# A planned two-layer kernel: other transfer latencies in its planner, the first V rows behind the output weights, another stored order

## The chip, the cores and the metric

The kernel runs on one core of a Trainium2 chip. The metric is the device time of one execution in microseconds (us); the time given for a kernel is the median of several executions. A "profiled execution" is one execution taken by the hardware profiler; its span runs from the first to the last instruction, and every duration below comes from it.

## The reference

Four layers follow one another on a sequence x of 2048 rows of 512 numbers (bf16): A, B, A, B, each added to its input, each on a layer norm of it.

```python
# A: recurrent attention with a memory of 8 rows; 64 segments of 32 rows, 32 heads of 128
mem = mem0
for s in range(64):
    h = concatenate([mem, x[s*32:(s+1)*32]])          # 40 rows
    q, k, v = h @ Wq, h @ Wk, h @ Wv                  # 40 x 4096 each
    p = softmax(mask(q @ k.T * scale))                # 40 x 40 for each head
    o = (p @ v) @ Wo                                  # 40 x 512
    mem, out[s] = o[:8], o[8:]
# B: a gated feed-forward net (FFN) with 1792 hidden columns
out = (sigmoid(x @ w_gate) * (x @ w_up)) @ w_down
```

The new memory of a segment needs the whole segment before it, so layer A is a chain of 64 steps. Both A layers have the same weights, and both B layers too.

## The kernel before

**Steps and jobs.** The kernel runs the two A layers as two jobs, j = 0 and j = 1, with job 1 six segments behind job 0 (LAG). One step t computes segment t of job 0 and segment t - 6 of job 1 side by side, so that most matmuls have 80 columns (two times 40). There are 70 steps: steps 0 to 5 and 64 to 69 have one job alone. After each fourth step a block of 128 rows goes through the FFN (`ffn`).

**A step** (`emit_step`) goes through six groups of heads. For each: q and k (L926), copied to qku by ScalarE; the scores (L961); the softmax on VectorE and ScalarE (L975 to L992); a transpose of the probabilities (L1004), whose two halves are spread into ptsb by ScalarE or VectorE (L1008 to L1017); probabilities times V (L1030, "pv") into a bank; and the output product with wo_sb (L1048), which adds up in one bank over all groups. The last product gives the memory of the next step (L1061, L1066).

**V** comes by two ways into the tiles vsb, of which there are three, two for each step (8 head pairs each). Rows of x that are known early go through `v_pass` (L716) or `v_half` (L753) to a DRAM buffer scr, and are fetched back for the step as **V rows** (L895, vsb<-scr, 16 or 48 KB a transfer). Rows that depend on the memory, and some next to them, are computed in the step itself as **V strips** (`strips`, L840: 32 columns for all heads) and copied into the tile sst by ScalarE or VectorE; four or eight DMAs (L906, vsb<-sst) take them to vsb. L1030 needs rows and strips.

**Weights.** wq, wk, wv and wo (4 MB each) are loaded once at the start (L603), in pieces: wo_sb in twelve, two for each of six groups of heads, ten of 384 KB and two of 128 KB. The last of them, in program text, is that of head 31. The FFN weights don't stay; GpSimd (POOL) issues their loads of 256 KB (wg, wu, wd, L1142, L1143, L1167) for each block anew. All other DMAs are issued by SyncE (SP), in the order of its instruction stream: where one of them waits for a semaphore, all behind it wait.

**The order of everything** is a plan made on the host before the program is built. `Planner.add` enters each of 13,442 tasks (a few instructions each) with the engines that may run it, a duration, a latency until its result is there, and what it reads and writes. `forward` then runs through time: whenever an engine is free, it takes the ready task that stands first in a stored order (SEQUENCE, a packed permutation of all tasks). The starts that come out give each engine's instruction order. Nothing of the modelled times is in the program: an engine waits only for the real semaphores of its data. Two exceptions are made from the plan: FFN loads wait for the matmul task that ended last before their planned start (`pace`), and where the plan has TensorE idle for over 250 ns, matmuls on a tile of zeros are put in (L1273, `warm`), to keep its clock up; their number follows from the planned gap.

A transfer with a size (`nb`) is modelled by one shared bus: it is done at the later of the bus's end plus 1.2 us and the end of its issue plus `lat`. FFN loads (at least BIG bytes on POOL) start only when the modelled bus is nearly free.

Of the kernel before, what the change touches and what calls it, by code (L numbers as in the profile page):

```python
# [1352 lines left out]
```

## Time and profile before

| what | us |
|---|---|
| median of 3 runs | 1787.03 |
| lowest and highest | 1783.6, 1788.61 |
| the profiled execution, its own time | 1788.62 |
| its span, first to last instruction | 1786.8 |
| TensorE busy in it | 1757.7 |
| TensorE matmuls on zeros (L1273) in it | 25.3 |
| VectorE, ScalarE, GpSimd busy | 1178.8, 1155.2, 581.9 |

TensorE's granted clock was 0.997 of full speed over the span. The profile names an instruction by its line, its engine (PE is TensorE's matmul, PEld its weight load, DVE VectorE, ACT ScalarE, POOL GpSimd, SPq SyncE's queue of DMA issues) and the tiles that it writes and reads ("vsb<-sst"). "Waits" list, for an engine, the line that waited, what released it, the sum of the waits, their number and the longest. The "chain" is the work that ended last, followed back from the end; a DMA in it lasts from the end of its issue until its landing.

### The profile page before, as it was taken

To read this page: it belongs to the slowest core of one execution; us is meant where nothing else is said; L and a number is where in the kernel's file an instruction comes from. 1 tells how busy PE (TensorE), PEld (TensorE's weight loads), DVE (VectorE), ACT (ScalarE), POOL (GpSimd) and SP (SyncE) were. 2 spreads that over 40 slices of the span, in tenths; PEclk is the share of its full clock that TensorE was granted. 3 is DMA by queue.
4 is the path that set the end of the run, shared out by engine and by line. 5 is a ranking of instruction groups with operands and counts; after the bars stand their busy time and mean duration, and the time that the engine had idled before them with its cause. 6 is when DMAs were issued, how large, how long until landed. Compare 5 with 4: busy or idle time off the path is not lost.

```text
span 1786.8 us, 92278 instructions
## 1 busy us (share of the span) xinstructions
PE 1757.7 (98%) x40059; PEld 1511.0 (85%) x40059; DVE 1178.8 (66%) x4061; ACT 1155.2 (65%) x2981; POOL 581.9 (33%) x839
## 2 busy tenths in 40 slices
PE   9999999999999999999999999999999999999998
PEld 4588788889888898989898898889888888989886
DVE  4377666776677666766676667657766766766675
ACT  5676756676666666666666666666665766666664
POOL 5414031413233242323334241333324132333432
PEclk9999999999999999999999999999999999999999
DMA  9735354636455464445546463545546454554543
GB/s 351 242 96 162 96 158 132 191 106 169 137 162 156 129 174 139 138 136 163 160 139 187 130 181 102 154 145 165 156 138 173 115 159 128 156 154 133 171 140 99
DMA packets 135048, 273.42 MB, mean 153 GB/s; under 512 B 30826, under 2 KB 68594, under 8 KB 134642
## 3 DMA queue, kind: packets, MB, share of 16 engines
q0 software_dynamic: 56848, 183.55, 35.0%
q1 hardware_dynamic: 77794, 83.97, 16.3%
q8 instruction: 314, 5.14, 1.3%
q14 instruction: 92, 0.75, 0.1%
HBM read 221.78 MB, written 27.07 MB: 139 GB/s over the span
## 4 chain that ended last, share of the span: by engine, by line
PE 89%; DMA 5%; SPq 2%; issue 1%; ACT 1%; DVE 1%; POOL 1%; POOLq 0%; ACTq 0%; DVEq 0%
PE bank L926 31%; PE bank L1048 16%; PE bank L1150 10%; PE bank L840 7%; PE bank L716 7%; PE bank L1173 5%; PE bank L1030 4%; PE bank L961 4%; PE bank L1004 2%; DMA vsb<-sst 2%; SPq L906 2%; DMA wv_sb<-in_A_Wv_dram 1%; PE bank L676 1%; DMA wo_sb<-in_A_Wo_dram 1%; PE bank L1118 0%
## 5 line engine op out<-in xcount | busy, mean ns | idle before, releaser
L926 PE MATMUL bank<-hT,wq_sb 128*128 128x80 bf16 (+3 forms) x8960 | 616.7, 198 | 1.2 <-issue 1.1
L926 PE MATMUL bank<-hT,wk_sb 128*128 128x80 bf16 (+3 forms) x8960 | 616.2, 198 | 0.5 <-issue 0.5
L1287 ACT CAST qku<-bank 128x480 bf16<-128x480 f32 (+3 forms) x770 | 387.8, 507 | 219.8 <-PE bank L926 180.9
L926 PEld LDWEIGHTS <-wq_sb 128*128 128x128 bf16 x8960 | 452.5, 99 | 23.7 <-issue 13.6
L926 PEld LDWEIGHTS <-wk_sb 128*128 128x128 bf16 x8960 | 447.7, 99 | 1.2 <-issue 1.2
L975 DVE TENSOR_TENSOR st<-bank,cst 40x240 f32<-40x240 f32 (+3 forms) x768 | 279.3, 368 | 155.6 <-PE bank L961 149.4
L1048 PE MATMUL bank<-otsb,wo_sb 128*128 128x80 bf16 (+1 forms) x8960 | 362.3, 198 | 5.5 <-DMA wo_sb<-in_A_Wo_dram 3.3
L1048 PEld LDWEIGHTS <-wo_sb 128*128 128x128 bf16 x8960 | 336.3, 99 | 18.8 <-DMA wo_sb<-in_A_Wo_dram 3.7
L1143 POOL DMA_DIRECT2D wu<-in_B_w_up_dram x217 | 164.6, 759 | 276.2 <-PE bank L1150 86.9
L1287 ACT CAST otsb<-bank 128x480 bf16<-128x480 f32 (+3 forms) x420 | 199.0, 484 | 68.1 <-PE bank L1030 48.2
L1142 POOL DMA_DIRECT2D wg<-in_B_w_gate_dram x217 | 163.9, 756 | 240.3 <-PE bank L1150 92.1
L1167 POOL DMA_DIRECT2D wd<-in_B_w_down_dram x217 | 154.2, 711 | 197.0 <-PE bank L1173 46.3
L985 ACT ACTIVATE st<-st 80x240 f32<-80x240 f32 (+3 forms) x420 | 158.9, 381 | 44.4 <-DVE st L982 42.8
L666 POOL TENSOR_TENSOR small<-small,cst 128x1 f32<-128x1 f32 (+1 forms) x80 | 45.7, 573 | 404.5 <-DVE small L665 401.6
L987 DVE TENSOR_REDUCE small<-st 80x6 f32<-80x240 f32 (+3 forms) x420 | 151.0, 362 | 37.3 <-ACT st L985 34.4
L1150 PE MATMUL bank<-xnT,wg 128*128 128x128 bf16 (+2 forms) x1784 | 171.9, 219 | 0.0
L1150 PE MATMUL bank<-xnT,wu 128*128 128x128 bf16 (+2 forms) x1784 | 171.3, 218 | 0.0
L961 PE MATMUL bank<-qku 128*128 128x80 bf16 (+1 forms) x2240 | 163.2, 198 | 1.4 <-ACT qku L1287 1.2
L982 DVE TENSOR_TENSOR st<-st,small 80x240 f32<-80x240 f32 (+3 forms) x420 | 154.6, 370 | 4.0
L992 DVE TENSOR_TENSOR pb<-st,small 80x240 bf16<-80x240 f32 (+3 forms) x420 | 153.4, 369 | 4.0
L980 DVE TENSOR_REDUCE small<-st 80x6 f32<-80x240 f32 (+3 forms) x420 | 151.6, 363 | 4.5
L1030 PE MATMUL bank<-ptsb,vsb 104*128 104x80 bf16 x2048 | 136.7, 199 | 7.8 <-DMA vsb<-sst 6.1
(106 smaller groups left out, 2403.4 us busy)
## 6 DMA issues: line engine op xcount, KB each, us to landing
wg<-in_B_w_gate_dram POOLq DMA_DIRECT2D x220, 256.0 KB, 4.4
wu<-in_B_w_up_dram POOLq DMA_DIRECT2D x220, 256.0 KB, 4.3
wd<-in_B_w_down_dram POOLq DMA_DIRECT2D x220, 256.0 KB, 4.2
vsb<-scr SPq DMA_DIRECT2D x460, 48.0 KB
vsb<-sst SPq DMA_DIRECT2D x464, 32.0 KB
scr<-vst SPq DMA_DIRECT2D x112, 96.0 KB
wv_sb<-in_A_Wv_dram SPq DMA_DIRECT2D x8, 512.0 KB
wo_sb<-in_A_Wo_dram SPq DMA_DIRECT2D x10, 384.0 KB
```

The source lines that it names most:

```text
L926: nc.tensor.matmul(o_ap, lhsT=W[:, c, h * P:(h + 1) * P], rhs=mv(c), start=(c == 0), stop=(c == DC - 1))
L961: nc.tensor.matmul(s_all(SB)[:, w0 + i, :], lhsT=fview(qku[:, i, 0, 0:1], [(1, P)]), rhs=qku[:, i, 1, 0:ncol], start=True, stop=True)
L975: pl.add("DVE", dve_ns(n, True), lambda gsz=gsz, hs=hs, st=st, SB=SB, pj_=pj_, npj_=npj_, mk=mk, idx=idx: nc.vector.tensor_tensor(out=st[p ...
L982: pl.add("DVE", dve_ns(n), lambda gsz=gsz, hs=hs, st=st, mx=mx: nc.vector.tensor_tensor(out=st[pr, hs], in0=st[pr, hs], in1=mx[pr, hs].uns ...
L985: pl.add("ACT", act_ns(n), lambda hs=hs, st=st: nc.scalar.activation(out=st[pr, hs], in_=st[pr, hs], func=ACTF.Exp, scale=self.scale), r=s ...
L1030: nc.tensor.matmul(fview(OB[:, o:o + 1], [(ncol, 2), (1, L)]), lhsT=self.vsb[halves[u // 8]][0:64 + L, j, (u % 8) * P:(u % 8 + 1) * P], rh ...
L1048: nc.tensor.matmul(WB[:, c * ncol:(c + 1) * ncol], lhsT=self.wo[:, h, c * P:(c + 1) * P], rhs=otsb[:, hl, 0:ncol], start=(h == 0 and c == ...
L1142: pl.add("POOL", 760, lambda wg=wg, fs=fs: nc.gpsimd.dma_start(out=wg[:], in_=self.wgv[:, :, fs]), r=[("wo", self.H - 1)], w=[gk] + bt, la ...
L1143: pl.add("POOL", 760, lambda wu=wu, fs=fs: nc.gpsimd.dma_start(out=wu[:], in_=self.wuv[:, :, fs]), r=[("wo", self.H - 1)], w=[uk] + bt, la ...
L1150: nc.tensor.matmul(gu[:, 2 * i + k, 0:n], lhsT=W[:, c, i * P:(i + 1) * P], rhs=xnT[:, c, rw], start=(c == 0), stop=(c == DC - 1))
L1167: pl.add("POOL", 760, lambda wd=wd, ip=ip: nc.gpsimd.dma_start(out=wd[:], in_=self.wdv[:, 2 * ip:2 * ip + 2, :]), w=[dk] + (["boot"] if se ...
L1287: nc.scalar.copy(out=dst, in_=src)
```

## The change

The diff changes numbers of the planner, one dependency, and the stored order. No task is added or removed.

- A task has a new field `slow`. `forward` keeps `wbus`, the time until which the FFN loads under way occupy the bus, and adds `slow` times the rest of that (at most BACK, 2300 ns) to a transfer's latency.
- V rows: `lat` 4300 becomes 2425 with `slow` 1.0, so 2425 to 4725 ns. V strips: 3200 becomes 2800 with `slow` 0.6, so 2800 to 4180 ns.
- The V rows of step 0 also depend on the output weight load of head 31. This is a dependency of the plan: it decides where the rows stand on SP; the program has no wait for it.
- `warm`: TensorE counts as slow until 4400 ns instead of 8000, the first gap is counted from 1000 ns instead of 1200, and a gap is filled at 2.4 columns per ns for the part of it behind 4400 ns (before, 1.2 for every gap whose end lay before 8000 ns).
- The second half of the ptsb spread costs 52 ns more on VectorE in the plan.
- SEQUENCE is another permutation. Unpacked: 422 of the 13,442 places hold the same task; half of all tasks move by 13 places or fewer; among the first 1000 places the median move is 166, from place 3000 on it is 6 to 24. The twelve wo_sb loads stood at places 322 to 646 and stand at 170 to 520; the four V rows of step 0 stood at 356 to 572 and stand at 427 to 509; the V matmuls of the start (L716 on xvf) stood at 169 to 759 and stand at 68 to 548.

```diff
 SEQUENCE = r"""
...
 """
-    SPAN, COLD, WARM0 = 3413.0, 8000.0, 1200.0
+    SPAN, COLD, WARM0, BACK = 3413.0, 4400.0, 1000.0, 2300.0
...
-    def add(self, eng, dur, fn, r=(), w=(), lat=None, boost=0.0, use=(), late=0.0, nb=0):
+    def add(self, eng, dur, fn, r=(), w=(), lat=None, boost=0.0, use=(), late=0.0, nb=0, slow=0.0):
...
-        bus = 0.0
+        bus = wbus = 0.0
...
-                    done = max(bus + self.TAIL, end + tk.lat)
+                    done = max(bus + self.TAIL, end + tk.lat + tk.slow * min(max(wbus - now, 0.0), self.BACK))
+                    if e == "POOL" and tk.nb >= self.BIG:
+                        wbus = max(wbus, now + self.LEAD[e]) + tk.nb / self.BUS
...
-                cold = tk.start < self.COLD
+                cold = end < self.COLD
...
-                    n = int((gap - 120.0) * (1.2 if cold else 2.4)) // P
+                    n = int((gap - 120.0) * 2.4 - (min(tk.start, self.COLD) - end) * 1.2 * cold) // P
...
-                        r=[("vd", j, b, q, kk) for q in range(lo // 8, (lo + nx) // 8) for kk in (h0 // 4, h0 // 4 + 1)], w=[("vx", j, vh, i)], lat=4300.0, nb=nx * 2048)
+                        r=[("vd", j, b, q, kk) for q in range(lo // 8, (lo + nx) // 8) for kk in (h0 // 4, h0 // 4 + 1)] + ([("wo", self.H - 1)] if t == 0 else []), w=[("vx", j, vh, i)], lat=2425.0, nb=nx * 2048, slow=1.0)
...
-                        r=[(sb, 0), (sb, 1)], w=[(name, j, vh, i)], lat=3200.0, use=[sb], nb=nr * 2048)
+                        r=[(sb, 0), (sb, 1)], w=[(name, j, vh, i)], lat=2800.0, use=[sb], nb=nr * 2048, slow=0.6)
...
                 d["ACT"] += 93.0 * i
+                d["DVE"] += 52.0 * i
```

## The prediction

> **What bounds the kernel now.** I read the page's busy shares first, then the waits of PE (TensorE), then its timeline and clock around the longest wait, then SP's own timeline in that stretch, and last the chain of work at a late stall.
>
> ```profile
> span 1786.8 us, 92278 instructions
> PE 1757.7 (98%) x40059; PEld 1511.0 (85%) x40059; DVE 1178.8 (66%) x4061; ACT 1155.2 (65%) x2981; POOL 581.9 (33%) x839
> ```
>
> TensorE is busy for 1757.7 of 1786.8 us; VectorE and ScalarE are busy for two thirds. The matmuls of the reference are the same in both programs, so only two things can shrink: the 29.1 us in which TensorE is idle, and the warming matmuls of L1273 (25.3 us by the groups of lines: 9.2 us before 20 us, 8.9 us from 100 to 220 us, 4.3 us after 1650 us). Everything else can only be hidden better or worse.
>
> The waits of TensorE (engine, line, what released it: us in total, times, longest):
>
> ```profile
> PE bank L1030 <- DMA vsb<-sst: 6.1, 7, 2.0
> PE bank L1048 <- DMA wo_sb<-in_A_Wo_dram: 3.3, 1, 3.3
> PE bank L1118 <- ACT oxT L1287: 2.1, 6, 0.4
> PE bank L716 <- DMA wv_sb<-in_A_Wv_dram: 1.6, 1, 1.6
> ```
>
> Two are the change's subject: seven short waits for V strips over the whole run, and one wait for an output weight. By stretches, the idle time is 8.7 us before 110 us, 6.3 us from 120 to 300 us, 8.2 us from 300 to 1740 us, and 6.1 us at the end. The steady stage has hardly anything left.
>
> TensorE's timeline at the output weight (start, length):
>
> ```profile
> 80.04 0.26 PE L1048 MATMUL bank<-otsb,wo_sb 128*128 128x40 bf16 x4
> 83.61 1.12 PE L1048 MATMUL bank<-otsb,wo_sb 128*128 128x40 bf16 x28 [3.30 <-DMA wo_sb<-in_A_Wo_dram]
> 84.55 1.88 PE L716 MATMUL bank<-wv_sb,xvf 128*128 128x512 bf16 x4
> ```
>
> and busy time, granted clock, DMA share and GB/s of single microseconds there:
>
> ```profile
> 82.00:83.00 1.00, 0.00 (x0) 0.83 1.05 380
> 83.00:84.00 1.00, 0.39 (x12) 0.50 0.72 248
> 84.00:85.00 1.00, 1.00 (x24) 0.50 0.20 61
> 88.00:89.00 1.00, 1.00 (x28) 0.50 0.55 129
> 89.00:90.00 1.00, 1.00 (x36) 0.75 0.39 133
> ```
>
> The wait costs more than its 3.30 us: the clock falls to 0.50 and comes back only at about 89.5 us. SP's timeline says why the weight was late:
>
> ```profile
> 54.12 0.37 SPq L603 DMA_DIRECT2D wo_sb<-in_A_Wo_dram  x1
> 54.53 2.74 SPq L895 DMA_DIRECT2D vsb<-scr  x2
> 67.62 2.61 SPq L906 DMA_DIRECT2D vsb<-sst  x3
> 70.28 0.59 SPq L603 DMA_DIRECT2D wo_sb<-in_A_Wo_dram  x1
> 70.91 0.52 SPq L906 DMA_DIRECT2D vsb<-sst  x1
> 71.47 2.69 SPq L603 DMA_DIRECT2D wo_sb<-in_A_Wo_dram  x5
> ```
>
> SP issues in order. After the V rows it stands at a strip's DMA (L906) from 57.3 to 67.6 us until the strip is in sst; six of the twelve output weights are behind it. Meanwhile the DMA engines run empty: 0.99 busy in 50 to 60 us, 0.32 (99 GB/s) in 60 to 70 us.
>
> Last, the chain of work at the longest strip wait:
>
> ```profile
> 1155.02 0.59 SPq L906
> 1155.61 0.04 issue
> 1155.65 4.85 DMA vsb<-sst
> ```
>
> A strip took 4.85 us from the end of its issue; at the other stalls that the chain shows it took 4.47, 4.58 and 5.57 us. The plan of before reckons with 3.2 us.
>
> **Step 1: output weights ahead of the first V rows.** The four V rows of step 0 now depend, in the plan, on the load of heads 31; the program gets no wait by it, only another order on SP. In the stored order the twelve weight loads stood at places 322 to 646 and now stand at 170 to 520. The six late ones (6 issues, 0.59 + 2.69 = 3.28 us of SP) should then go out before SP blocks, by about 54.5 + 3.3 = 58 us. They are 2.0 MB (five of 384 KB, one of 128 KB, by the old order). At the 365 to 395 GB/s of the busy stretches that is 5.3 to 5.8 us, from about 60 us, when the DMA engines come free: landed near 66 us instead of 83.56. The need is at 76 to 80 us, so the 3.30 us go.
>
> The clock: after 83.61 us four matmuls of L716 take 1.67 us to the next group where they took 0.86 at 79.18 us (+0.81); 28 of L1048 take 0.94 where 0.71 is the warm pace of 24 in 0.61 (+0.23); the 18 pairs of L926 from 86.22 to 89.49 us take 3.27 where the warm pace later is 0.10 for a group of four, 1.8 in all (+1.45). Sum 2.5 us. Here the Trainium skill speaks against counting it: TensorE: Matmul & The Clock Gate, Part 1, has the clock fall after at least one idle window of about 3.4 us, and the wait was 3.30 us. By that rule only 3.30 us would be won; by the row, 3.30 + 2.5 = 5.8 us. The row decides, since it shows 0.50.
>
> What is late next is the V rows, moved behind six weight issues: four issues (1.9 us for four at 51.21 us) between 66 and 68 us at the earliest. The first L1030 comes at 74.86 us, and its strips, issued from 67.6 to 71.4 us, land last anyway. So I cost the move at nothing, hidden by L716, L926 and L753 work until 74.8 us. If the weights land only at 70 us, the rows land at 72.5 to 76.5 us (2.4 to 4.7 us after issue, the change's own figures) and up to 1.7 us show. I take +0.5, bounds 0 and 4.7. POOL's FFN loads, which the plan also ties to head 31, find their weights earlier; FFN of block 0 starts only after step 3, so that is worth nothing.
>
> **Step 2: strip latency 3.2 to 2.8 + 0.6 of the FFN load under way.** With the cap of 2300 ns it is 4.18 us at most, 0.98 more than before where a load runs. All the stalls have DMA shares of 0.42 to 0.88 around them with FFN loads. If the plan puts the matmuls 0.98 us later, behind other work, the waits of 2.0, 1.3, 0.7, 0.7, 0.7, 0.4 and 0.2 us shrink to 1.0, 0.3 and zeros: 4.8 us of 6.1 gone, for the plan has other matmuls to put there (TensorE is 98% busy). Where no load runs, 2.8 is less than 3.2: bounds 0 and +3 (0.1 to 0.2 us at one step in four), I take +0.5.
>
> **Step 3: V rows 4.3 to 2.43, up to 4.73 under a load.** No wait of before is for a row (vsb<-scr), so nothing can be won directly; the plan may move pv matmuls up to 1.9 us nearer to the rows. The Trainium skill (DMA: Bandwidth & Descriptors, Anatomy of one DMA) gives about 2.0 us and bytes over 436 GB/s, fitted to transfers issued by GpSimd: an estimate of 2.1 us for 48 KB, so 2.43 would be safe and the step costs 0. The nearest row, strips of 32 KB on the same SP queue, shows 4.47 to 5.57 us, though in the worst cases and under loads: against 4.73 there, the shortfall is up to 0.8 us. Sum by the rule 0; by the row, a few steps at 0.8 us, 16 us at worst (rival B). Rows mostly wait for a buffer that L1030 releases (SP's wait L895 for L1030, 365.3 us in 89 times), long before use, so I lean to the rule: +2.
>
> **Step 4: warming matmuls.** COLD falls from 8.0 to 4.4 us, and time after it is filled at 2.4 columns per ns instead of 1.2. The trace agrees: the weight loads of the first 16 fillers come every 0.42 us until 4.28 us, then every 0.21. A filler of the same planned gap gets longer: TensorE's 1.03 us of idle before 7.09 us gets filled, and the first transposes, at 10.36 us, may come up to 0.9 us later. TensorE stands 1.64 us for a V weight at 28.8 us, which hides that: 0, bounds 0 and +0.9 (with the 1.64 gone, it shows). Nothing is won there, as the first data set the pace.
>
> **Step 5: ptsb spread +52 ns on VectorE, and the order.** No instruction is added. The 240-wide DVE form takes 331 ns against 270 for the plain copy, so the plan gets nearer to the trace; VectorE has a third free: 0. The order moves half of the tasks by 13 places or fewer; in the first 1000 places the median is 166. All V matmuls of the start (L716, former places 169 to 759) now stand by place 548, so they no longer pad the gaps of steps 1 to 5, where 8.9 us of fillers and 6.3 us of idle already are. That can cost (+4) or, with gaps planned otherwise, gain (-4); a reordering has new misfits. I take +0.7.
>
> Sum: -5.8 + 0.5 - 4.8 + 0.5 + 2 + 0 + 0.7 = -6.9 us. On the profiled execution, 1788.6 us (span 1786.8 and 1.8 around it), that gives 1781.7. The median shown is 1787.0, 1.6 below it: 1780.1.
>
> **Rivals.** A, about the same, 1783 to 1792: the weight's 5.8 us are won, but the strip waits only change places (the new cap of 4.18 us is still under all four landings of 4.47 to 5.57), and the start's gaps take the rest; 1787.0 - 5.8 + 4 = 1785. For it speaks that a plan fitted to measured latencies left 24 us of waits before, too. Against it: the steady stage's waits are few enough to be met one by one. It includes the case that the weights don't move, because SP's list, and no wait in the program, decides, and another blocked strip stands ahead of them.
>
> B, slower, at about 1797: V rows planned too tightly. Of 64 steps with rows, if one in four finds them 1 us late, that is 16 us, less 6.9 won: 1796. The place is L1030 waiting for vsb<-scr, from 200 us on. It decides from about 7 us of such waits, that is once unloaded rows land later than about 3.4 us. For it: transfers on this queue were seen at 4.5 us and above. Against it: those are the late ones only, and no wait for rows is in the trace.
>
> **How the numbers follow.** Forecast, faster (1774 to 1781.6): 0.48. Rival A and other cases within 0.3%: 0.30. Rival B and other slower cases: 0.22. 0.3%, 5.4 us, is about what a measurement of this kernel can tell from no change. The range 1771 to 1797 leaves out the tail of B (fewer than 2 in 10) and a gain beyond 16 us. The forecast's own range is 1774 to 1781.6.
>
> **What would show it.** Right: no wait of L1048 for wo_sb and clock 1.00 in 80 to 90 us; SP's last wo_sb issue before about 60 us, with V rows after it; vsb<-sst waits of 2 us or less in all; fillers about 25 us. Wrong: L1030 waiting for vsb<-scr, the wo_sb issues still behind a blocked L906, or more fillers and idle time between 100 and 300 us than the 8.9 and 6.3 us of now.

## The result, and the profile after

| | median us | runs | lowest to highest |
|---|---|---|---|
| before, beside it on the same chip | 1786.79 | 20 | 1780.75 to 1793.32 |
| after | 1789.00 | 20 | 1783.69 to 1798.83 |

The ratio after to before is 1.0013, interval 1.0002 to 1.0025. Forecast was 1780.1 and "faster"; the kernel became slower by about 2 us, a time that lies within rival A's 1783 to 1792. Beside later experiments the same program gave 1.0018 (1.0008 to 1.0028). The profiled execution of after took 1786.9 us of its own time, 2.1 below its median; that of before took 1788.6, 1.8 above its median. So the two profiles stand to each other as the medians do not, and I took a second profile of each program, unchanged, called "second" below.

The page of after (first profile):

```profile
span 1785.1 us, 92363 instructions
PE 1762.3 (99%) x40081; PEld 1510.4 (85%) x40081; DVE 1171.3 (66%) x4002; ACT 1170.9 (66%) x3040; POOL 575.6 (32%) x831
```

TensorE's idle time fell from 29.1 to 22.8 us, but it is busy for longer with the same matmuls. The fillers on the tile of zeros ("hot") grew. Their group in after, all shapes together (behind the first bar: busy us, mean ns of one):

```profile
L1271 PE MATMUL bank<-hot 128*128 128x512 bf16 (+3 forms) x107 | 27.6, 375 | 1.0 <-DVE small L573 1.0
```

The same group of before has 22.4 us, so fillers took 5.2 us more. (The 25.3 us of the prediction are the sum over single shapes, which overlap.)

What TensorE waited for (us in total, times, longest), after:

```profile
PE bank L1028 <- DMA vsb<-sst: 3.1, 8, 0.8
PE bank L1028 <- DMA vsb<-scr: 2.6, 3, 1.9
PE bank L1116 <- ACT oxT L1285: 1.8, 5, 0.4
PE bank L1046 <- ACT otsb L1285: 1.8, 3, 1.4
```

(Lines have moved by 2 or 3: L1030 is L1028 now, L1048 L1046, L716 L713, L906 L903, L895 L892, L603 L600, L1066 L1064.) The wait for wo_sb is gone and a wait for V rows is new. The second profile of after has the new wait again and no gain at the strips:

```profile
PE bank L1028 <- DMA vsb<-sst: 7.8, 13, 1.5
PE bank L1028 <- DMA vsb<-scr: 3.0, 2, 2.7
```

The second profile of before:

```profile
PE bank L1030 <- DMA vsb<-sst: 3.7, 8, 1.0
PE bank L1048 <- DMA wo_sb<-in_A_Wo_dram: 2.2, 1, 2.2
```

Waits for strips: 6.1 and 3.7 us in before, 3.1 and 7.8 in after. One pair of profiles would have shown a gain of 3.0 us that the other pair turns round. Over all profiles of this document, the six with before's constants and order have 3.7 to 9.8 us (mean 5.8) and the seven with after's 2.5 to 7.8 (mean 4.2); some of these have their start edited.

The output weights on SP, after:

```profile
57.98 2.27 SPq L600 DMA_DIRECT2D wo_sb<-in_A_Wo_dram  x4
64.40 1.85 SPq L903 DMA_DIRECT2D vsb<-sst  x3
66.29 0.58 SPq L600 DMA_DIRECT2D wo_sb<-in_A_Wo_dram  x1
71.45 0.67 SPq L892 DMA_DIRECT2D vsb<-scr  x2
```

Ten of the twelve pieces are out at 60.3 us, ahead of the strips, as step 1 had it; two follow only at 66.3 and 77.3 us. The V rows of step 0, issued from 51.2 us on in before, come at 71.5 us and later. TensorE waits for none of these. The clock (busy time of the stretch, granted clock, DMA share, GB/s) in after stays full there:

```profile
80.00:82.00 2.00, 2.00 (x57) 1.00 1.07 363
82.00:84.00 2.00, 2.00 (x85) 1.00 1.00 344
```

and yet step 0 doesn't end sooner. The instruction that writes the memory for the next step shows where steps end; here it is for the first two steps (min/median/max ns, then the start of the first and the last), in before:

```profile
L1066 DVE CAST hT<-bank x2: 191/192/192, 85.1 to 106.9; 128x32 bf16<-128x32 f32 x2
```

and in after:

```profile
L1064 DVE CAST hT<-bank x2: 192/192/192, 86.1 to 103.3; 128x32 bf16<-128x32 f32 x2
```

Step 0 ends 1.0 us later although 3.3 us of stall and the low clock are gone; step 1 ends 3.6 sooner, and at step 5's end 1.2 us of that are left (179.8 to 178.6). Why is seen at the V matmuls of the start from 60 us on, before:

```profile
L716 PE MATMUL bank<-wv_sb,xvf x61: 376/379/634, 59.8 to 99.7; 128*128 128x512 bf16 x61
```

and after:

```profile
L713 PE MATMUL bank<-wv_sb,xvf x69: 376/379/389, 59.8 to 80.3; 128*128 128x512 bf16 x69
```

In before 20 of them run from 84.55 us on, in the gaps of step 1, where a single job leaves TensorE with nothing else; in after all 69 stand ahead of step 0's end. From 59.7 to 84.5 us TensorE is busy with them for 16.25 us (71 of them) in after and 10.01 us in before. The gaps get fillers instead. The busy time of L1271 in stretches, after:

```profile
80.00:100.00 20.00, 2.39 (x9) 1.00 0.49 153
100.00:120.00 20.00, 3.60 (x17) 1.00 0.32 86
```

against 0 and 3.24 us of L1273 in before.

The planner's own promise can be laid beside this, once it is run on the host with both programs (plan), and the four profiles (trace; first, second; here the start of the memory write, 0.2 us before its end):

| end of, us | plan before | plan after | trace before | trace after |
|---|---|---|---|---|
| step 0 | 78.9 | 84.3 | 85.1, 83.9 | 86.1, 85.8 |
| step 1 | 98.0 | 101.4 | 106.9, 104.7 | 103.3, 103.0 |
| step 5 | 169.6 | 173.5 | 179.8, 176.5 | 178.6, 178.2 |
| step 15 | 414.2 | 418.0 | 429.8, 425.2 | 426.0, 426.1 |
| step 19 | 516.1 | 520.4 | 532.0, 527.4 | 530.1, 532.7 |
| step 20 | 541.6 | 546.4 | 557.5, 552.9 | 556.3, 559.4 |
| step 68 | 1723.4 | 1728.7 | 1750.8, 1742.7 | 1749.2, 1754.0 |
| all | 1755.5 | 1760.4 | 1786.8, 1779.4 | 1785.1, 1788.7 |

The new plan promises step 0 5.4 us later than the old one, and the end 4.9 us later. It keeps its promise better (at step 1 it is 1.8 us late on average, the old one 7.8), and the two nearly cancel. Each plan is made with its own latencies, so the 4.9 us are not the price of the order alone.

At the ends of steps 3, 7, 11, 15 and so on, TensorE has done the same matmuls in both programs, fillers left out, so there the two can be compared. (In between they can't: step 18 takes 32.3 us in after and 25.7 in before, mostly because matmuls of steps 16 and 17 have moved into it.) On the mean of the two profiles, after is 0.4 to 1.6 us ahead from step 3 to step 15, and 1.7 us behind at the end of step 19. Steps 16 to 19 of the first profiles (stretch, its length, TensorE busy, clock, DMA share, GB/s), before and after:

```profile
429.80:531.95 102.15, 101.79 (x2297) 1.00 0.54 154
425.97:530.06 104.09, 102.92 (x2297) 1.00 0.53 153
```

The second profiles have 102.1 and 106.5 us. New waits for V rows are 0.7 and 2.7 us of this; the rest, over 1 us in each, is no wait of size: the same 2297 matmuls take longer in the other order. This repeats: the six profiles with before's constants and order have 102.1 to 102.5 us here, the seven with after's 103.5 to 106.5. Steps 20 to 23 take 101.2 us in each of the six and 101.8 to 102.9 us in the seven.

### The profile page after: what moved, and what is told of

Same layout as the page of the kernel before. It is cut to its first block, busy times and chain, and to the rows that moved or that the text cites. A ratio compares the mean times of both kernels' runs of the same rounds, so it can differ in the third digit from the quotient of the medians.

```text
span 1785.1 us, 92363 instructions
## 1 busy us (share of the span) xinstructions
PE 1762.3 (99%) x40081; PEld 1510.4 (85%) x40081; DVE 1171.3 (66%) x4002; ACT 1170.9 (66%) x3040; POOL 575.6 (32%) x831
## 4 chain that ended last, share of the span: by engine, by line
PE 91%; DMA 3%; DVE 2%; SPq 2%; ACT 1%; issue 1%; POOL 0%; ACTq 0%; POOLq 0%
PE bank L923 30%; PE bank L1046 17%; PE bank L1148 11%; PE bank L713 8%; PE bank L837 7%; PE bank L1171 5%; PE bank L1028 4%; PE bank L958 4%; PE bank L1001 2%; DMA vsb<-sst 2%; SPq L903 2%; PE bank L1271 1%; PE bank L673 1%; PE bank L1116 0%; DMA kx<-xq 0%
## 5 line engine op out<-in xcount | busy, mean ns | idle before, releaser
L1285 ACT CAST qku<-bank 128x480 bf16<-128x480 f32 (+4 forms) x770 | 387.5, 507 | 220.2 <-PE bank L923 183.0
L972 DVE TENSOR_TENSOR st<-bank,cst 40x240 f32<-40x240 f32 (+2 forms) x768 | 277.4, 367 | 169.7 <-PE bank L958 162.8
L1046 PE MATMUL bank<-otsb,wo_sb 128*128 128x80 bf16 (+1 forms) x8960 | 363.5, 198 | 3.3 <-ACT otsb L1285 1.8
L1046 PEld LDWEIGHTS <-wo_sb 128*128 128x128 bf16 x8960 | 336.8, 99 | 18.5 <-issue 3.8
L1028 PE MATMUL bank<-ptsb,vsb 104*128 104x80 bf16 x2048 | 138.3, 199 | 6.5 <-DMA vsb<-sst 3.1
```

The source lines that it names most:

```text
L972: pl.add("DVE", dve_ns(n, True), lambda gsz=gsz, hs=hs, st=st, SB=SB, pj_=pj_, npj_=npj_, mk=mk, idx=idx: nc.vector.tensor_tensor(out=st[p ...
L1028: nc.tensor.matmul(fview(OB[:, o:o + 1], [(ncol, 2), (1, L)]), lhsT=self.vsb[halves[u // 8]][0:64 + L, j, (u % 8) * P:(u % 8 + 1) * P], rh ...
L1046: nc.tensor.matmul(WB[:, c * ncol:(c + 1) * ncol], lhsT=self.wo[:, h, c * P:(c + 1) * P], rhs=otsb[:, hl, 0:ncol], start=(h == 0 and c == ...
L1285: nc.scalar.copy(out=dst, in_=src)
```

## The experiments

**My theory** from these profiles: the stall's removal works, but the plan pays for it by V matmuls too early (at the start), rows just in time (later), and a start with too many fillers; the strips gain nothing. **Rivals**: the stall was never worth 5.8 us; the loss lies in the steady stage's strips; the loss lies in the clock. All kernels are compared with runs of before made beside them on the same chip, since before's own median lay between 1784.15 and 1788.13 us there. The ratio is worked out from the single runs; it is not the quotient of the two medians and differs from it by up to 0.0011, or 2 us (a_v_back: 0.9999 as a quotient). Where the two disagree, the ratio with its interval counts. The last column is the granted clock, as the mean over the runs, with that of before beside them in brackets (once for each median of before).

| kernel | median us (runs) | before | ratio, interval | span of the profile | clock |
|---|---|---|---|---|---|
| b_wo_early | 1784.00 (14) | 1786.29 | 0.9993, 0.9978 to 1.0007 | 1780.9 | 0.9983 (0.9978) |
| b_hot_stall | 1787.38 (22) | 1786.29 | 1.0009, 0.9997 to 1.0022 | 1790.6 | 0.9987 |
| a_v_back | 1786.09 (14) | 1786.29 | 1.0010, 0.9996 to 1.0023 | 1782.6 | 0.9984 |
| a_trim | 1789.86 (20) | 1786.29 | 1.0021, 1.0010 to 1.0033 | 1785.9 | 0.9990 |
| rep_before | 1784.36 (14) | 1785.79 | 0.9994, 0.9983 to 1.0005 | 1779.4 | 0.9981 (0.9980) |
| rep_after | 1788.57 (22) | 1785.79 | 1.0018, 1.0008 to 1.0028 | 1788.7 | 0.9990 |
| rep_wo_early | 1783.08 (14) | 1785.79 | 0.9988, 0.9975 to 1.0002 | 1779.6 | 0.9986 |
| b_newlat | 1810.61 (4) | 1785.79 | 1.0142, 1.0121 to 1.0163 | 1807.9 | 0.9990 |
| a_rows | 1788.13 (22) | 1788.13 | 1.0000, 0.9987 to 1.0012 | 1787.0 | 0.9995 (0.9977) |
| a_rows_v | 1785.83 (13) | 1788.13 | 0.9997, 0.9986 to 1.0008 | 1783.0 | 0.9990 |
| rep_v_back | 1788.27 (14) | 1788.13 | 1.0003, 0.9990 to 1.0015 | 1782.9 | 0.9984 |
| b_wo_tail | 1784.84 (14) | 1784.15 | 0.9997, 0.9983 to 1.0011 | 1782.6 | 0.9990 (0.9984) |

**b_wo_early** and **rep_wo_early**: step 1 of the prediction alone, in before.

```diff
         order = self.pl.plan()
+        at = min(k for k, tk in enumerate(order) if tk.idx in self.strip0)
+        late = [tk for tk in order[at:] if tk.idx in self.wos]
+        order = order[:at] + late + [tk for tk in order[at:] if tk.idx not in self.wos]
```

(`wos` are the loads of wo_sb, `strip0` the strip DMAs of step 0.)

> The kernel before, in which only SP's order is altered: the output weight loads that stood behind the first V strip of step 0 are issued just ahead of it. Theory (the stall is worth what the prediction said, and the changed kernel spent it elsewhere): no wait of L1048 for wo_sb, clock 1.00 from 80 to 90 us, step 0 over at about 80 instead of 85 us, time 5 to 6 us less than before (ratio about 0.997). Rival (the stall only hid another one: strips, rows or the softmax chain end at the same point): the idle time comes back under another name within steps 0 and 1, time within 2 us of before.

> Before with the last output weights issued ahead of the first strips on SP, once more. Theory: ratio 0.998 to 1.0000, step 0 over near 81 us, no wait for the output weights; the end 1.5 to 6 us below that of before's profiles. Rival: the first profile's 5.9 us was luck in the strips, and the ratio is 1.000 or above.

Measured: the wait for wo_sb is gone, the clock is 1.00 from 80 to 90 us, and steps 0 and 1 end at 81.1 and 100.3 us:

```profile
L1068 DVE CAST hT<-bank x2: 192/192/192, 81.1 to 100.3; 128x32 bf16<-128x32 f32 x2
```

That is 4.0 and 6.6 us sooner than in the first profile of before, 2.8 and 4.4 sooner than in the second. The medians are 2.3 and 2.7 us below before; by the ratios it is 1.3 and 2.1 us, and both intervals include 1. So the edit gains about what the rival allowed (within 2 us), and that it gains at all is likely but not clear of noise. One place where the lead shrinks is the stretch from 200 to 310 us of b_wo_early:

```profile
PE bank L1050 <- ACT otsb L1293: 2.6, 2, 1.6
PE bank L963 <- ACT qku L1293: 1.5, 1, 1.5
PE bank L1006 <- DVE pb L994: 1.0, 1, 1.0
```

These waits for ScalarE's copies and VectorE's softmax (otsb, qku, pb) are 5.1 us here, against 3.1 and 1.2 (otsb and qku; none for pb) in the two profiles of before. Against the second profile of before the lead is 2.8 us at step 5 and nothing at step 10 (301.3 to 300.8); in rep_wo_early 1.0 us is left there (299.8). That an earlier chain must wait so is read from these profiles; no run tests it.

**b_hot_stall**: before with 14 filler matmuls in the stall, so that the clock stays up and the weight still comes late.

```diff
+                if tk.idx == self.stall:
+                    for _ in range(14):
+                        nc.tensor.matmul(self.bank.tiles[7][:, 0:4 * P], lhsT=self.hot[:], rhs=fview(self.hot[:, 0:1], [(0, 4), (1, P)]), start=True, stop=True)
                 got = tk.fn()
```

> The kernel before with 14 matmuls of 512 columns on a tile of zeros put in front of the matmuls that stall for the output weight; the weight comes as late as before. If the clock's fall costs the 2.5 us that the prediction counted: clock 1.00 after 83.6 us, the same landing of the weight near 83.5 us, time 2 to 2.5 us less than before. If only the 3.30 us of idle count (the clock would have come back beside other waits): time within 1 us of before.

Measured: step 1 ends at 103.4 us, 3.5 and 1.3 sooner than in before, yet the median is no better (1.0009). In its profile the clock fell elsewhere, at 220 us (busy, clock, DMA share, GB/s):

```profile
218.00:220.00 2.00, 0.50 (x15) 0.99 0.35 117
220.00:222.00 2.00, 1.66 (x26) 0.50 0.03 8
222.00:224.00 2.00, 1.79 (x28) 0.50 0.00 0
```

So a warm clock at 82 us alone is worth nothing that the median shows.

**rep_before** and **rep_after**: both programs once more.

> The kernel before, unchanged, once more. Theory: the ratio to itself is 1.000 within 0.0015; the profile again shows the wait for the output weights (3 to 4 us, once) and a clock under full after it, step 0 over near 85 us. The waits for strips (6.1 us in the first profile, 9.8 in the run with warm fillers at the same order) differ by several us from execution to execution, so a single pair of profiles does not carry a difference of under 4 us. Rival: the first profile was typical, the strips' waits come out within 1 us of 6.1 and the span within 1.5 us of 1786.8.

> The kernel after, unchanged, once more. Theory: its ratio to before is 1.0005 to 1.0025 again; the profile has no wait for the output weights, step 0 over at 86 to 87 us although nothing stalls in it, and waits for strips and V rows that sum to 5 to 7 us; the fall of the clock near 1774 us is a matter of the execution and need not come back. Rival: the strips' and rows' waits fall under 3 us or the clock falls again at the same place, so that the first profile's tail is a fixed part of the order.

Measured: before against itself is 0.9994, so about 0.1% is noise; after is slower again, and its waits for strips and rows sum to 10.8 us, above the 5 to 7 expected. The stall of before was 2.2 us this time, and the clock fell for half as long:

```profile
82.00:84.00 2.00, 1.29 (x30) 0.92 0.96 341
84.00:86.00 2.00, 2.00 (x28) 0.50 0.18 55
86.00:88.00 2.00, 2.00 (x65) 0.73 0.42 113
```

Summed over such stretches, (1 - clock) times their length, the two profiles lost 3.4 us and 1.7 us to this fall; I had taken 2.5 us from the first. The first profile of after lost 1.7 us near 1774 us; in the second that fall is not there, but one at 1574 us:

```profile
1574.00:1576.00 2.00, 1.78 (x21) 0.55 0.23 39
1576.00:1578.00 2.00, 2.00 (x30) 0.59 0.67 203
```

So the falls of one program differ between executions, though some come back: the one behind 1766 us in the second profile of before is in both of b_wo_early, too, and not in the first of before. Over all runs the clock lacks 0.0016 to 0.0023 of full speed in before (two falls of 1.7 us in 1784 us make 0.0019) and 0.0008 to 0.0010 in after. The change does keep the clock up; it loses the time elsewhere.

**b_newlat**: the planner's new constants alone, with before's stored sequence.

```diff
-    SPAN, COLD, WARM0 = 3413.0, 8000.0, 1200.0
+    SPAN, COLD, WARM0, BACK = 3413.0, 4400.0, 1000.0, 2300.0
...
-w=[("vx", j, vh, i)], lat=4300.0, nb=nx * 2048)
+w=[("vx", j, vh, i)], lat=2425.0, nb=nx * 2048, slow=1.0)
...
-w=[(name, j, vh, i)], lat=3200.0, use=[sb], nb=nr * 2048)
+w=[(name, j, vh, i)], lat=2800.0, use=[sb], nb=nr * 2048, slow=0.6)
```

(and the rest of the diff of the change but for the dependency and SEQUENCE.)

> Before with the planner's new constants alone (strips 2.80 us plus 0.6 of what lies ahead of them, V rows 2.43 us plus all of it, no start under 4.4 us as cold, the FFN transfers counted), and before's stored sequence of priorities. The planner's own end moves from 1755.5 to 1794.2 us. Theory: constants and sequence belong together; re-planned so, tasks keep their rank but wait for later due times, so the time rises, by less than the 39 us of the plan, since the strips do land later than before's plan held: the median is 1795 to 1815. The waits for strips are under 2 us, the idle time and fillers instead rise. Rival: what the plan says costs nothing on the chip, only the order counts: the median within 6 us of before.

Measured: 1.4% slower. The strips' waits fell, and others took their place:

```profile
PE bank L1052 <- ACT otsb L1291: 7.6, 15, 1.1
PE bank L1034 <- DMA vsb<-sst: 2.8, 5, 1.2
PE bank L1052 <- DMA wo_sb<-in_A_Wo_dram: 2.2, 1, 2.2
```

and its group of fillers:

```profile
L1277 PE MATMUL bank<-hot 128*128 128x512 bf16 (+3 forms) x139 | 37.6, 373 | 1.0 <-DVE small L579 1.0
```

Strips 2.8 us (under 2 expected), but fillers 37.6 us (before 22.4 and 22.9). A longer latency in the plan doesn't bring the strip sooner; it moves the matmul, and the place is then empty unless the sequence has something for it. Constants and sequence are one thing.

**a_trim**: after with 4 fillers of 512 columns fewer at the start (`n -= 16` for the first gap).

> The changed kernel with its first run of fillers shortened by 16 units of 128 columns (four matmuls of 512, 0.86 us). Theory (the fillers of the new rule end after the first normalized rows are there): the first transposes start near 10.4 instead of 10.9 us, the first V matmul near 12.1 instead of 12.8, and step 0 ends about 0.6 us sooner. Rival (the V weights' transfer sets that stretch): a wait for wv_sb or xn of the same size takes its place, and step 0 ends where it did, at 86 us.

Measured: no gain. In after the first row block was normalized at 9.84 + 0.41 us, but the fillers ended only at 11:

```profile
1.00 10.08 PE L1271 MATMUL bank<-hot 128*128 128x512 bf16 x38 [1.00 <-DVE small L573]
10.91 0.39 PE L673 MATMUL bank<-cst,xn 128*128 128x128 bf16 x4
12.80 1.04 PE L713 MATMUL bank<-wv_sb,xvf 128*128 128x512 bf16 x4
```

The first V matmul is 0.8 us later than in before (11.99); between the second profiles it is 0.5 us (12.55 to 12.06). In a_trim's profile it came at 13.10: there the fillers kept to 0.43 us each until 7 us, where in after the faster pace begins between 4 and 5 us, so 4 fillers fewer took as long, and the data came 0.5 us later too (10.3). The edit was lost in what varies between executions, so it doesn't tell what the longer fillers cost.

**a_v_back** and **rep_v_back**: after, with two V units of the start (four groups of four V matmuls with their copies and stores, 12 tasks) moved behind step 0, into gaps of steps 1 and 2, and no fillers planned from 60 to 80 us.

```diff
         order = self.pl.plan()
+        for i, at in {355: 111450.0, 356: 112550.0, 357: 112350.0, 358: 113450.0, 359: 114150.0, 360: 114150.0, 339: 100750.0, 340: 101850.0, 337: 117950.0, 338: 119050.0, 341: 119700.0, 342: 119700.0}.items():
+            self.pl.tasks[i].start = at
...
+        order.sort(key=lambda k: (k.start, k.idx))
```

> The changed kernel with two V units (four groups of four V matmuls, their copies and stores) taken from before the end of step 0 and put into gaps of steps 1 and 2, where fillers stood (101, 111 to 113 and 118 us of the plan); no filler is put into the places that they leave. Theory (V matmuls that no longer pad the gaps of steps 1 to 5 cost the changed kernel 3 to 4 us): step 0 ends 2 to 3.4 us sooner, steps 1 to 2 take no longer, time 2 to 3.4 us less than the changed kernel, so about 1 us less than before (ratio 0.9995). Rival (those gaps are no longer than the matmuls' neighbours need, or the copies on ScalarE delay the chain): step 0 ends sooner, but step 2 ends where it did; ratio about 1.001.

> After with the V blocks of the start moved back into the gaps of steps 1 and 2, once more. Theory: step 0 over at 84 to 85 us, ratio 1.000 to 1.0015, so 1.5 to 3 us below after. Rival: the first run was luck, the ratio is that of after (1.0013 to 1.0018).

Measured, the memory writes of steps 0 and 1 in a_v_back:

```profile
L1064 DVE CAST hT<-bank x2: 191/192/192, 84.3 to 101.2; 128x32 bf16<-128x32 f32 x2
```

Both are about 2 us sooner than in after, fillers from 80 to 180 us fall from 10.7 to 7.3 us, and the profiles end at 1782.6 and 1782.9 instead of 1785.1 and 1788.7. The end of step 2 is still 1.2 to 1.6 us sooner. The ratios, 1.0010 and 1.0003, are below after's 1.0013 and 1.0018, with intervals that overlap; the first is what the rival expected, the second lies in the theory's range.

**a_rows**: after, with two V blocks swapped at two places so that a row can be fetched sooner.

```diff
+        for p, q in ((3341, 3353), (6391, 6395)):
+            x, y = self.pl.tasks[p:p + 4], self.pl.tasks[q:q + 4]
+            for k, m in zip(x, y):
+                k.start, m.start = m.start, k.start
+            for k, m in zip(x[0].acq, y[0].acq):
+                k.slot, m.slot = m.slot, k.slot
+        self.pl.tasks[3728].start, self.pl.tasks[6789].start = 481820.0, 882670.0
```

The place, in the second profile of after: SP writes V blocks to scr, three strips go out, and the rows are issued only at 496.53 us,

```profile
493.10 0.57 SPq L1281 DMA_DIRECT2D scr<-vst  x1
493.72 2.77 SPq L903 DMA_DIRECT2D vsb<-sst  x3
496.53 14.16 SPq L892 DMA_DIRECT2D vsb<-scr  x13
```

and TensorE stands at the mix for 2.65 us:

```profile
500.47 0.57 PE L1028 MATMUL bank<-ptsb,vsb 104*128 104x80 bf16 x11 [2.65 <-DMA vsb<-scr]
```

The chain of the first profile of after says how long these rows took from issue to landing, here and at the second place:

```profile
497.08 4.40 DMA vsb<-scr
901.80 3.97 DMA vsb<-scr
```

The plan has 2.43 us for a row, and the smallest distance from a row's issue to its matmul in the plan is 2.8 us in after (four are under 4 us), 4.7 us in before.

> After with two V blocks of the same kind swapped in the order at two places (step 18 and near 890 us), so that the V row that the mix there needs is written 4 to 8 us sooner, and this row load moved ahead of the strips on SP. In all four profiles of after's order so far the mix waited there for a row (0.7, 2.7, 0.7, 2.2 us at step 18; 1.9, 0.3, 2.3, 0.2 us near 890 us), and in none of before's. Theory: the plan's 2.43 us for a row put it just in time, and it lands later; with the row sooner the waits for rows fall from 2.4 to 3.0 us to under 0.7 us in all, step 18 takes 30.5 to 31.7 us instead of 32.1 to 34.1, and the median falls by 1 to 3 us against after, to a ratio of 0.9995 to 1.0010. Rival: the waits are taken over by the strips that the row load passes on SP, the rows' waits vanish and the strips' grow by as much, and the ratio stays at 1.0015 to 1.002.

Measured: the waits for rows are 0.3 us in all, so the cause of that wait is shown. It is not the whole loss at this place: steps 16 to 19 take 105.1 us, as long as in after (104.1, 106.5). Step 18 took 32.6 us, not 31.7 or less (32.3 and 34.1 in after), the strips' waits are 5.3 us, and the profile ends at 1787.0, between the two of after. The ratio is as expected, 1.0000, but its interval overlaps those of after.

**a_rows_v**: both edits.

> After with the V blocks of the start moved back into the gaps of steps 1 and 2 (as in a_v_back) and with the two rows sooner (as in a_rows). Theory: the two losses are at different places and add up: step 0 over near 84.3 us, waits for rows under 0.7 us, median 1783 to 1785.5, a ratio of 0.998 to 0.9995, level with before that has its output weights sooner. Rival: beyond a_v_back nothing is gained (1.000 to 1.001), since a later wait takes it.

Measured: step 0 over at 84.4 us; the ratio, 0.9997, lies between what theory and rival expected, and above b_wo_early's, but its interval (0.9986 to 1.0008) no more than touches after's (1.0008 to 1.0028). What TensorE waits for at the mix now:

```profile
PE bank L1028 <- DMA vsb<-sst: 2.6, 5, 1.3
PE bank L1028 <- issue: 1.8, 2, 1.4
```

So a few tasks moved in the order, at the start and at two later places, bring the time level with before's, with no constant changed; that this is better than after is only just clear of noise. Steps 16 to 23 stay longer than before's here, too (103.5 and 102.2 us against 102.1 and 101.2).

**b_wo_tail**: b_wo_early with 8 more fillers in the tail, meant to beat both kernels.

```diff
             fill = self.pl.warm(order)
+            fill[13403] = (fill[13403][0], 20)
+            fill[13391] = (fill[13403][0], 16)
```

> Before with the last output weights ahead of the first strips (as in b_wo_early) and with 8 more filler matmuls of 512 columns in the two idle stretches of 0.95 and 1.2 us of the tail, at 1764 and 1766 us, behind which the clock stood at half speed for 3.4 us in both profiles of that kernel. Theory: such a fall costs up to 1.7 us; with the stretches filled the clock stays full there, the tail from the last memory write to the end shortens from 36.9 and 37.1 us to 35.5 to 36.3, the mean clock of the runs rises from 0.9983 and 0.9986 to 0.999 or more, and the ratio is 0.998 to 0.999. Rival: the tail is bound by the chain of the last blocks, not by the matmuls at half clock; the clock is full and the tail as long as before, ratio 0.999 to 1.0.

Measured: the tail is full at clock and 36.0 us long (1746.6 to 1782.6) instead of 36.9 and 37.1. But in this profile the clock fell at another place (busy, clock):

```profile
66.00:68.00 2.00, 1.11 (x11) 0.72 1.05 389
68.00:70.00 2.00, 1.93 (x24) 0.50 0.82 291
```

step 0 ended 3.7 to 4.1 us later than in b_wo_early's profiles, and the ratio is the rival's. No version beats before by more than its interval; b_wo_early is the nearest.

## Why the prediction was wrong, step by step

**Step 1, output weights (-5.8, +0.5 for the rows).** The mechanism was right: no wait, full clock, first rows not missed, though two of the weights still went out after 60 us. The size was wrong: alone it gives 1.3 and 2.1 us by the ratios, 2.3 and 2.7 by the medians. The two terms, 3.30 us of wait and 2.5 us of clock, came from one execution; the second had 2.2 us and half the fall. And the prediction had no term for giving back: b_wo_early and its repeat are 5.2 us ahead of before at the end of step 3 and 2.2 us at the end of step 15. "I cost the move at nothing" held for the rows.

**Step 2, strips (-4.8, +0.5).** This step failed. "The waits ... shrink to 1.0, 0.3 and zeros" reckoned each wait of one trace as a fixed thing that a later place removes. In good part they are the scatter of landings: 3.7 to 9.8 us in the six profiles with before's order, 2.5 to 7.8 in the seven with after's. Of the 4.8 us, the difference of the means leaves 1.6, and that is not clear of the scatter. "The plan has other matmuls to put there" was counted as free; b_newlat, all the new constants with before's sequence, is 1.4% slower.

**Step 3, V rows (+2).** Right in mechanism and size: waits for vsb<-scr of 2.6 and 3.0 us, by rows that took 4.40 and 3.97 us (3.89 and 3.33 in the second profile) and not 2.43. Here the row of the trace (strips, 4.47 to 5.57 us) was the better guide; the estimate of 2.1 us from the Trainium skill (DMA: Bandwidth & Descriptors, Anatomy of one DMA) lies 1.2 to 2.3 us below what these four rows took. Rival B's mechanism is thus real, at two places instead of sixteen, under the 7 us from which it decides.

**Step 4, fillers (0 to +0.9).** The first V matmul is 0.8 and 0.5 us late, near the upper bound. Whether the kernel's end pays for it is open: a_trim didn't move it, and the wait for a V weight that was to hide it (1.6 and 0.7 us in before) is gone in after.

**Step 5, order (+0.7, bounds -4 and +4).** The second failing term. It named the right thing, the V matmuls that "no longer pad the gaps", and priced it, with all "new misfits", at a sixth of its bound. The runs show two costs in its place. At the end of step 0, 20 V matmuls more stand ahead, about 4.6 us (an estimate from 16.25 us for 71), and all the stall's gain has gone; a_v_back takes back 1.8 to 2.1 us there. And from step 16 on the new order is slower in the steady stage. Here is by how much each kernel is ahead (+) or behind (-) of before at steps with equal work (us, means of both profiles where there are two):

| kernel | step 3 | step 15 | step 19 | step 23 | step 68 |
|---|---|---|---|---|---|
| after | +1.6 | +1.5 | -1.7 | -2.5 | -4.8 |
| b_wo_early | +5.2 | +2.2 | +2.0 | +2.0 | +3.5 |
| a_v_back | +2.8 | +3.3 | +1.8 | +0.4 | -0.7 |
| a_rows | +0.2 | -1.9 | -4.8 | -5.9 | -5.5 |
| a_rows_v | +2.4 | +0.7 | -0.6 | -1.6 | -1.3 |

The values themselves scatter by some us: the two profiles of before lie 8.0 us apart at step 68. But the drop from step 15 to step 23 is in every kernel with the new order and not in b_wo_early. Waits for rows are a part of it (0.7 and 2.7 us in after); a_rows drops without them. Why the same matmuls take longer there stays open.

A sum of single edits, -2.5 (step 1, by the medians), 0 (step 2), +2 to +3 (step 3), +0.8 (step 4) and +2 (a_v_back's share of step 5), makes +2.3 to +3.3 us, near the measured +2.2 and +2.8. That is luck: the sum mixes medians with single profiles, its terms are uncertain by 1 to 2 us each, and the steady stage's loss beside the rows is not in it. What is shown is that step 1's edit removes the stall, that the new order loses 2.5 and 5.5 us from step 16 to step 23 in the two profiles of after, and that a_rows and a_v_back together bring the time level with before's. Not settled is how the whole loss divides.

Rival A came nearest. Its first part, that the weight's 5.8 us are won, doesn't hold; "the strip waits only change places" and "the start's gaps take the rest" describe a part of what happened, and the steady stage's loss is in neither of its reasons.

## What to carry to other kernels

When a stall is removed by another order, ask what the work that now stands ahead padded before: in front of a serial chain it delays the chain (here 20 V matmuls ate the gain of a stall of 3.3 us), in the chain's gaps it costs less. A latency in a plan doesn't make a transfer sooner, so raising it pays only where the order has work for the freed place. And before a wait of a few us is written into a sum, look at it in a second profile of the same program: here the same waits were 6.1 and 3.7 us, and the stall 3.3 and 2.2. Compare two orders where they have done the same work: where nothing waits for a DMA, such a stretch can repeat to 0.1 us (101.2 us for steps 20 to 23 in all six profiles with before's order), so it shows a loss of 1 us that whole runs can't.

## What was not expected of the hardware

In these profiles the clock fell for 3.4 us at half speed, which costs up to 1.7 us, or for twice that, at places that differ between executions of one program. It also fell without one long idle stretch: in the second profile of b_wo_early at 1766 us, after idle times of 0.95 and 1.20 us with work between them. The Trainium skill (TensorE: Matmul & The Clock Gate, Part 1) gives a window of about 3.4 us, which agrees with the length of a fall; that a whole idle window comes first doesn't agree with this row, nor with the 2.2 us of the second profile of before. Busy time in the 2 us before the low clock:

```profile
1764.00:1766.00 2.00, 0.85 (x3) 1.00 0.56 150
1766.00:1768.00 2.00, 1.66 (x46) 0.66 0.65 166
```

Filling the clock's hole doesn't by itself win time: b_hot_stall had a higher mean clock than before and the same time.
